# Linear attention beside a spatial gating MLP: moving the attention and its k, v, q projections to other places in the program

## The chip, the cores and the metric

The kernel runs on one core of a Trainium2 chip. The metric is the device time of one execution in microseconds (us). All times come from the chip; spans, waits and clocks come from the profile of one execution each. Every run that is used here counts as a fast run, except the control, of which there is a single run and so no state.

## The reference

```python
def reference(A_x, A_wqkv, A_wo, B_x, B_w_in, B_w_sp, B_b_sp, B_w_out):
    x = A_x                                     # [1, 2048, 576], bf16
    xn = _layernorm(x, axis=-1)
    s = _A_ref(xn, A_wqkv, A_wo)                # attention, 32 heads of 18
    g = _silu(_B_ref(xn, B_w_in, B_w_sp, B_b_sp, B_w_out))
    return x + s * g
# _A_ref: phi(t) = where(t > 0, t + 1, exp(t)) + 1e-6
#   kv = sum_s phi(k) v^T, z = sum_s phi(k); o = phi(q) kv / (phi(q) z + 1e-6); o @ wo
# _B_ref: z = gelu(xn @ w_in); z1, z2 = halves of 2304; z2 = layernorm(z2)
#   g = w_sp @ z2 + b_sp; (z1 * g) @ w_out
```

Two branches share the normalised input and meet only in the last line. Both are stated in bf16.

## The kernel before

The program works on 16 tiles of 128 rows. Its first stage makes, tile after tile, the transposed input `xnT`, the k/v projection (`stage_C`) and the z2 half of the input projection (`stage_D`) with its normalisation (`E1`, `E2`). Then come the sum over all rows (`kvacc`), and the attention by itself: `stage_Q` (q projection), `stage_N` (numerator and denominator), `stage_O`, `stage_R` (transpose) and `stage_W` (times wo). Last comes what is called stage 4 here: z1, g and b. (PSUM, below, is the memory that the matmuls of this program write to, in pieces called banks; SBUF is the one that its other tiles lie in, HBM the one that its inputs, scratch and output lie in.)

```python
    xc0 = ...                                                    # first x chunk, 4 tiles
    load_rows126(nc.sync, Win2[:, :, f0:f0 + fn], ...)           # first of five pieces
    load_rows126(nc.sync, Wkv[:, :, 0:D], A_wqkv, D, 2 * D)
    load_rows126(nc.sync, Wkv[:, :, D:2 * D], A_wqkv, 2 * D, 3 * D)
    for (f0, fn) in fch[1:]:
        load_rows126(nc.sync, Win2[:, :, f0:f0 + fn], ...)
    load_x(1)                                                    # second x chunk
    ...
    for t in range(NS):                                          # NS = 16
        maybe(stage_A1, t + 4)      # statistics of x            (VectorE)
        maybe(stage_A2, t + 3)      # xn                         (VectorE)
        maybe(stage_B, t + 2)       # transposes, xnT            (TensorE, ScalarE)
        maybe(stage_C_pe, t + 1)    # k/v matmuls into one tile of 3 PSUM banks
        maybe(stage_C_act, t + 1)   # Exp, copies of v           (ScalarE)
        maybe(stage_E1, t - 1)      # statistics of z2           (VectorE)
        maybe(stage_E2, t - 2)      # z2 normalised              (VectorE)
        maybe(stage_C_dve, t + 1)   # pk                         (VectorE)
        stage_D(t)                  # 25 z2 matmuls, 5 Gelus     (TensorE, ScalarE)
    ...
    load_rows126(nc.sync, Wqq[:, :, :], A_wqkv, 0, D)            # into a pool opened here
    ...  # kvacc: 5 groups of 16 matmuls, each group evicted before the next
    for j in range(J):                                           # J = 5
        stage_Q(0, j)
    for i in range(NS + 2):
        # stage_Q of the next chunk, N(i), R(i-1), O(i), W(i-2)
        ...
    # stage 4: for each of 4 column chunks z1, g (16 k steps), b; out = x + silu(b) * A_sb
```

Of the kernel before, what the change touches and what calls it, by code (L numbers as in the profile page):

```python
# [28 lines left out]
def kernel(  # L29
# [32 lines left out]
    EPS_LN = 1e-5  # L62

# [3 lines left out]

    consts = ctx.enter_context(tc.tile_pool(name="consts", bufs=1, side="left"))
    big = ctx.enter_context(tc.tile_pool(name="big", bufs=1, side="left"))
    z2p = ctx.enter_context(tc.tile_pool(name="z2p", bufs=1, side="right"))  # L70
# [9 lines left out]
    mask2d = mask[:].rearrange("p a b -> p (a b)")  # L80
    neg_half = consts.tile([P, 1], F32, name="neg_half")
# [3 lines left out]
    z2 = z2p.tile([P, NS, Fh], BF16, name="z2")  # L85
# [4 lines left out]
    pkp_ctx = ExitStack()  # L90
    pkp = pkp_ctx.enter_context(tc.tile_pool(name="pkp", bufs=NS, side="left"))
    p1_sb = ExitStack()
    p1_ps = ExitStack()
    wp1 = p1_sb.enter_context(tc.tile_pool(name="wp1", bufs=1, side="left"))
    Wkv = wp1.tile([P, J, 2 * D], BF16, name="Wkv")
    Win2 = wp1.tile([P, J, Fh], BF16, name="Win2")
    xcp = p1_sb.enter_context(tc.tile_pool(name="xcp", bufs=2, side="left"))
    stg1 = p1_sb.enter_context(tc.tile_pool(name="stg1", bufs=3, side="left"))
    sm1 = p1_sb.enter_context(tc.tile_pool(name="sm1", bufs=6, side="left"))
    ps_t = p1_ps.enter_context(tc.tile_pool(name="ps_t", bufs=1, space=PSUM))  # L100
    ps_kv = p1_ps.enter_context(tc.tile_pool(name="ps_kv", bufs=1, space=PSUM))
    ps_z = p1_ps.enter_context(tc.tile_pool(name="ps_z", bufs=4, space=PSUM))

    fch = _chunks(Fh, 512)
    sch = _chunks(Fh, 384)
# [12 lines left out]
    (f0, fn) = fch[0]  # L118
    load_rows126(nc.sync, Win2[:, :, f0:f0 + fn], B_w_in, Fh + f0, Fh + f0 + fn)
    load_rows126(nc.sync, Wkv[:, :, 0:D], A_wqkv, D, 2 * D)  # L120
    load_rows126(nc.sync, Wkv[:, :, D:2 * D], A_wqkv, 2 * D, 3 * D)
    for (f0, fn) in fch[1:]:
        load_rows126(nc.sync, Win2[:, :, f0:f0 + fn], B_w_in, Fh + f0, Fh + f0 + fn)
    if SC > 1:
        load_x(1)

# [17 lines left out]
    def stage_A2(i):  # L144
        xt, mv, rstd = st_a.pop(i)
        xn = stg1.tile([P, DPAD], BF16, name="xn")
        nc.gpsimd.memset(xn[:, D:DPAD], 0.0)
        nc.vector.tensor_scalar(out=xn[:, 0:D], in0=xt, scalar1=mv[:, 0:1], scalar2=rstd[:, 0:1],
                                op0=ALU.subtract, op1=ALU.mult)
        xn_tiles[i] = xn  # L150
        c, ii = divmod(i, 4)
        if ii == 3 and c + 2 < SC:
            load_x(c + 2)
# [10 lines left out]
    def stage_C_pe(i):  # L164
        pkv = ps_kv.tile([P, 3, 512], F32, name="pkv")
        groups = [(0, 0, 0, 288), (1, 0, 288, 288), (2, 0, D, 4 * GW), (1, 288, D + 4 * GW, JSZ[4])]
        for (b, o, w0, n) in groups:
            for j in range(J):
                nc.tensor.matmul(out=pkv[:, b, o:o + n], lhsT=xnT[0:JSZ[j], j, i * P:(i + 1) * P],  # L169
                                 rhs=Wkv[0:JSZ[j], j, w0:w0 + n], start=(j == 0), stop=(j == J - 1))  # L170
        c_state[i] = pkv

    def stage_C_act(i):
        pkv = c_state[i]
        e = stg1.tile([P, 2, 288], F32, name="e_k")
        nc.scalar.activation(out=e[:], in_=pkv[:, 0:2, 0:288], func=ACT.Exp)
        va = pkp.tile([P, J, GW + 1], BF16, name="va")
        nc.gpsimd.memset(va[:, 0:4, GW:GW + 1], 1.0)
        nc.gpsimd.memset(va[:, 4, JSZ[4]:JSZ[4] + 1], 1.0)
        nc.scalar.copy(out=va[:, 0:4, 0:GW], in_=pkv[:, 2, 0:4 * GW].rearrange("p (j e) -> p j e", j=4))  # L180
        nc.scalar.copy(out=va[:, 4, 0:JSZ[4]], in_=pkv[:, 1, 288:288 + JSZ[4]])
        va_tiles[i] = va
        c_state[i] = (pkv, e)

    def stage_C_dve(i):
        pkv, e = c_state.pop(i)
        nc.vector.tensor_scalar(out=e[:], in0=e[:], scalar1=1.0, scalar2=1e-6, op0=ALU.min, op1=ALU.add)
        pk = pkp.tile([P, D], BF16, name="pk")
        nc.vector.scalar_tensor_tensor(out=pk[:].rearrange("p (b n) -> p b n", b=2), in0=pkv[:, 0:2, 0:288], scalar=0.0,
                                       in1=e[:], op0=ALU.max, op1=ALU.add)  # L190
        pk_tiles[i] = pk

# [10 lines left out]
    def stage_E1(i):  # L203
        st = sm1.tile([P, len(sch), nc.vector.BN_STATS_DIM], F32, name="st3")
        for si, (f0, fn) in enumerate(sch):
            nc.vector.bn_stats(out=st[:, si, :], in_=z2[:, i, f0:f0 + fn])  # L206
        mv = sm1.tile([P, 2], F32, name="mv3")
        nc.vector.bn_aggr(out=mv[:], in_=st[:])
        rstd = sm1.tile([P, 1], F32, name="rstd3")
# [9 lines left out]
    def maybe(fn, i):  # L219
        if 0 <= i < NS:  # L220
            fn(i)

    with tc.high_priority():
        stage_A1(0)
        stage_A2(0)
        stage_B(0)
    for i in range(1, min(4, NS)):
        stage_A1(i)
    for i in range(1, min(3, NS)):
        stage_A2(i)  # L230
    maybe(stage_B, 1)
    stage_C_pe(0)
    stage_C_act(0)
    stage_C_dve(0)
    for t in range(NS):
        maybe(stage_A1, t + 4)
        maybe(stage_A2, t + 3)
        maybe(stage_B, t + 2)
        maybe(stage_C_pe, t + 1)
        maybe(stage_C_act, t + 1)  # L240
        maybe(stage_E1, t - 1)
        maybe(stage_E2, t - 2)
        maybe(stage_C_dve, t + 1)
        stage_D(t)
    stage_E1(NS - 1)
    maybe(stage_E2, NS - 2)
    stage_E2(NS - 1)

    p1_ps.close()
    p1_sb.close()  # L250

    p2_r = ExitStack()
    asbp = ctx.enter_context(tc.tile_pool(name="asbp", bufs=1, side="right"))
    A_sb = asbp.tile([P, NS, D], BF16, name="A_sb")
    bep = p2_r.enter_context(tc.tile_pool(name="bep", bufs=1, side="right"))
    rhsj = bep.tile([P, J, NW], BF16, name="rhsj")
    Wqq = bep.tile([P, J, D], BF16, name="Wqq")
    Wo = bep.tile([P, J, D], BF16, name="Wo")
    pqT = bep.tile([P, J, S], BF16, name="pqT")
    load_rows126(nc.sync, Wqq[:, :, :], A_wqkv, 0, D)  # L260
    load_rows126(nc.sync, Wo[:, :, :], A_wo, 0, D)

    p2_ps = ExitStack()
    ps_q = p2_ps.enter_context(tc.tile_pool(name="ps_q", bufs=2, space=PSUM))

    with tc.tile_pool(name="ps_kvacc", bufs=1, space=PSUM) as ps_kvacc, tc.tile_pool(name="sm2a", bufs=2, side="left") as sm2a:
        kvacc = ps_kvacc.tile([P, J, 512], F32, name="kvacc")
        for j in range(J):
            nj = JSZ[j]
            for i in range(NS):  # L270
                nc.tensor.matmul(out=kvacc[0:nj, j, 0:nj + 1], lhsT=pk_tiles[i][:, j * GW:j * GW + nj],
                                 rhs=va_tiles[i][:, j, 0:nj + 1], start=(i == 0), stop=(i == NS - 1))
            nc.vector.tensor_tensor(out=rhsj[0:nj, j, 0:nj], in0=kvacc[0:nj, j, 0:nj], in1=mask2d[0:nj, 0:nj], op=ALU.mult)
            zc = sm2a.tile([P, 1], F32, name="zc")
            nc.vector.tensor_copy(out=zc[0:nj], in_=kvacc[0:nj, j, nj:nj + 1])
            nc.vector.tensor_scalar(out=rhsj[0:nj, j, nj:nj + JH[j]], in0=mask[0:nj, 0:JH[j], 0], scalar1=zc[0:nj, 0:1], scalar2=None,
                                    op0=ALU.mult)
    pkp_ctx.close()

    spw = ctx.enter_context(tc.tile_pool(name="spw", bufs=1, side="left"))  # L280
    Win1 = spw.tile([P, J, Fh], BF16, name="Win1")
    wT_tiles = {}

    def load_wT(c):
        t = spw.tile([P, NS, 512], BF16, name="wT")
        nc.sync.dma_start_transpose(out=t[:], in_=B_w_sp[c * 512:(c + 1) * 512, :])
        wT_tiles[c] = t

    p2_sb = ExitStack()
    stg2 = p2_sb.enter_context(tc.tile_pool(name="stg2", bufs=3, side="left"))  # L290
    sm2 = p2_sb.enter_context(tc.tile_pool(name="sm2", bufs=4, side="left"))
    ps_nd = p2_ps.enter_context(tc.tile_pool(name="ps_nd", bufs=1, space=PSUM))
    ps_ot = p2_ps.enter_context(tc.tile_pool(name="ps_ot", bufs=2, space=PSUM))
    ps_a = p2_ps.enter_context(tc.tile_pool(name="ps_a", bufs=1, space=PSUM))

    def stage_Q(c, j):
        nj = JSZ[j]
        pq_ps = ps_q.tile([P, 512], F32, name="pq_ps")
        for kt in range(J):
            nc.tensor.matmul(out=pq_ps[0:nj, :], lhsT=Wqq[0:JSZ[kt], kt, j * GW:j * GW + nj],  # L300
                             rhs=xnT[0:JSZ[kt], kt, c * 512:(c + 1) * 512], start=(kt == 0), stop=(kt == J - 1))
        e = stg2.tile([P, 512], F32, name="e_q")
        nc.scalar.activation(out=e[0:nj, :], in_=pq_ps[0:nj, :], func=ACT.Exp)  # L303
        nc.vector.tensor_scalar(out=e[0:nj, :], in0=e[0:nj, :], scalar1=1.0, scalar2=1e-6, op0=ALU.min, op1=ALU.add)  # L304
# [173 lines left out]
```

## Time and profile before

| | before |
|---|---|
| median of the first 4 runs | 612.01 us (610.53 to 612.80) |
| span of the profiled run (610.53 us) | 608.8 us |
| mean granted TensorE clock in it | 0.994 |
| TensorE / VectorE / ScalarE busy | 584.2 / 253.0 / 209.0 us |
| moved by DMA | 27.14 MB |

The profile is of one run, here the fastest of the four. That matters when its span is set against a median.

Two readings bear on the argument and are not in the prediction. The first is of the seam between first stage and attention. In the chain of waits (start, length, what held the end), VectorE finishes the last z2 tile, and then the load of the q weights is on the path for 4.41 us: its buffer came free only there.

```profile
142.31 0.89 DVE z L216
...
143.33 4.41 DMA Wqq<-in_A_wqkv_dram
```

The timeline of TensorE (PE) at the same place (start, length, engine, line, form; in brackets the idle time before and what ended it) shows PE waiting between the groups of kvacc:

```profile
140.23 1.08 PE L271 MATMUL kvacc<-va,pk 128*126 128x127 bf16 x16 [0.47 <-ACT z L199]
143.69 1.84 PE L271 MATMUL kvacc<-va,pk 128*126 128x127 bf16 x16 [2.38 <-DVE zc L275]
...
149.03 0.81 PE L300 MATMUL pq_ps<-xnT,Wqq 126*126 126x512 bf16 x3
```

The second reading is of the groups of instructions on ScalarE. The loads of function tables (count, then busy us and ns of one, then idle time before) are many, but they lie on an engine that is not the bound:

```profile
L199 ACT ACT_TABLE_LOAD x16 | 20.5, 1283 | 0.3
L176 ACT ACT_TABLE_LOAD x15 | 19.2, 1283 | 0.3
```

### The profile page before, as it was taken

The page shows a single profiled execution, that of the slowest core. Times are in us where ns is not written, and L with a number is a line of the kernel's source. Part 1 is how long each engine was busy: PE and PEld are TensorE (multiplying, and loading weights), DVE is VectorE, ACT ScalarE, POOL GpSimd, SP SyncE. Part 2 cuts the span into 40 slices and gives each one's busy share as a digit, 9 for nine tenths or more (in the row PEclk, how much of TensorE's full clock was granted, in tenths as well). Part 3 has the DMA queues.
Part 4 walks back from the last instruction along what each step waited for, and adds up shares of the span by engine and source line. Part 5 has one row for each costly group of instructions (what it writes and reads, how often), then busy time and mean ns, then how long its engine had stood idle before and what let it go on. Part 6 is the DMA issues. An engine that isn't in the chain of part 4 may idle for free.

```text
span 608.8 us, 8283 instructions
## 1 busy us (share of the span) xinstructions
PE 584.2 (96%) x3468; PEld 321.2 (53%) x3468; DVE 253.0 (42%) x552; ACT 209.0 (34%) x325; POOL 26.7 (4%) x105
## 2 busy tenths in 40 slices
PE   3799999997899999999999999999999999999996
PEld 2455555555577644444754444574444475444465
DVE  4599777775776203323211332230233321123323
ACT  1799999982465550000242000135000024300011
POOL 3023000000001000000000000000000000000000
PEclk9999999998999999999999999999999999999999
DMA  8410000003910150000710000530000071000001
GB/s 247 132 39 2 1 2 1 0 2 91 290 23 1 56 193 1 1 1 1 177 40 1 0 1 0 118 88 12 0 1 1 1 176 41 1 1 0 1 0 40
DMA packets 48153, 27.14 MB, mean 45 GB/s; under 512 B 33780, under 2 KB 47412, under 8 KB 48116
## 3 DMA queue, kind: packets, MB, share of 16 engines
q1 hardware_dynamic: 48116, 26.61, 16.1%
q8 instruction: 27, 0.44, 0.3%
q14 instruction: 10, 0.08, 0.0%
HBM read 15.86 MB, written 2.36 MB: 30 GB/s over the span
## 4 chain that ended last, share of the span: by engine, by line
PE 91%; DVE 3%; issue 2%; DMA 2%; ACT 1%; POOL 0%; SPq 0%; POOLq 0%; ACTq 0%
PE g_ps L425 40%; PE z_ps L403 13%; PE b_ps L439 12%; PE zp L197 11%; PE pkv L169 7%; PE a_ps L360 3%; PE pq_ps L300 3%; PE pT L159 1%; DMA xc<-in_A_x_dram 1%; PE oT_ps L350 1%; PE nd L318 1%; DVE pqT L305 1%; DMA Wqq<-in_A_wqkv_dram 1%; DVE e_q L304 0%; ACT e_q L303 0%
## 5 line engine op out<-in xcount | busy, mean ns | idle before, releaser
L425 PE MATMUL g_ps<-wT,z 128*128 128x512 bf16 x1152 | 250.1, 379 | 0.0
L425 PEld LDWEIGHTS <-z 128*128 128x128 bf16 x1152 | 112.7, 98 | 135.8
L427 DVE TENSOR_TENSOR gb<-g_ps,b_bc 128x512 bf16<-128x512 f32 x72 | 49.8, 691 | 232.9 <-PE g_ps L425 207.6
L406 ACT ACTIVATE z<-z_ps 128x512 bf16<-128x512 f32 x72 | 42.6, 597 | 215.1 <-PE z_ps L403 215.0
L197 PE MATMUL zp<-Win,xnT 126*128 126x512 bf16 (+3 forms) x400 | 81.8, 358 | 0.0
L403 PE MATMUL z_ps<-xnT,Win 126*128 126x512 bf16 (+1 forms) x360 | 80.6, 379 | 0.2 <-DVE pqT L305 0.2
L439 PE MATMUL b_ps<-Wout,z 128*128 128x288 bf16 x576 | 71.2, 286 | 0.0
L439 PEld LDWEIGHTS <-z 128*128 128x128 bf16 x576 | 56.3, 98 | 15.0
L403 PEld LDWEIGHTS <-Win 126*128 126x128 bf16 (+1 forms) x360 | 34.9, 97 | 42.1 <-issue 0.8
L197 PEld LDWEIGHTS <-xnT 126*128 126x128 bf16 (+1 forms) x400 | 37.5, 97 | 36.9 <-issue 0.4
L206 DVE BATCH_NORM_STATS2 st<-z 128x6 f32<-128x384 bf16 x96 | 46.5, 549 | 13.0 <-ACT z L199 12.8
L169 PE MATMUL pkv<-Wkv,xnT 126*128 126x288 bf16 (+4 forms) x320 | 44.8, 296 | 3.2 <-DVE rstd L138 3.2
L199 ACT ACTIVATE z<-zp 128x512 bf16<-128x512 f32 (+1 forms) x80 | 40.9, 555 | 5.7 <-PE zp L197 5.3
L169 PEld LDWEIGHTS <-xnT 126*128 126x128 bf16 (+1 forms) x320 | 28.6, 101 | 18.8 <-issue 4.9
L444 DVE TENSOR_TENSOR sB<-sB,A_sb 128x576 f32<-128x576 f32 x16 | 12.1, 758 | 56.5 <-ACT sB L442 56.5
L428 DVE TENSOR_TENSOR z<-gb,z 128x512 bf16<-128x512 bf16 x72 | 30.6, 425 | 7.1
L442 ACT ACT_TABLE_LOAD x4 | 5.1, 1283 | 76.5 <-PE b_ps L439 76.5
L300 PE MATMUL pq_ps<-xnT,Wqq 126*126 126x512 bf16 (+3 forms) x100 | 24.5, 380 | 1.9 <-DVE pqT L305 1.6
L442 ACT ACTIVATE sB<-b_ps 128x576 f32<-128x576 f32 x16 | 10.4, 651 | 40.0 <-PE b_ps L439 32.5
L360 PE MATMUL a_ps<-Wo,oT 126*128 126x288 bf16 (+1 forms) x160 | 22.5, 285 | 0.0
L199 ACT ACT_TABLE_LOAD x16 | 20.5, 1283 | 0.3
L159 PE MATMUL pT<-ident,xn 128*126 128x128 bf16 x80 | 9.7, 232 | 10.4 <-POOL rstd L139 9.6
(58 smaller groups left out, 345.1 us busy)
## 6 DMA issues: line engine op xcount, KB each, us to landing
Wout<-in_B_w_out_dram SPq DMA_DIRECT2D x1, 2592.0 KB
x_r<-in_A_x_dram SPq DMA_DIRECT2D x16, 144.0 KB
out_dram<-ot SPq DMA_DIRECT2D x16, 144.0 KB
Win<-in_B_w_in_dram SPq DMA_DIRECT2D x1, 2268.0 KB
Win<-in_B_w_in_dram SPq DMA_DIRECT2D x4, 504.0 KB
xc<-in_A_x_dram SPq DMA_DIRECT2D x3, 576.0 KB
Wkv<-in_A_wqkv_dram SPq DMA_DIRECT2D x2, 567.0 KB
Wqq<-in_A_wqkv_dram SPq DMA_DIRECT2D x1, 567.0 KB
```

The costliest lines, as they stand in the source:

```text
L169: nc.tensor.matmul(out=pkv[:, b, o:o + n], lhsT=xnT[0:JSZ[j], j, i * P:(i + 1) * P], rhs=Wkv[0:JSZ[j], j, w0:w0 + n], start=(j == 0), stop ...
L197: nc.tensor.matmul(out=zp[:, 0:fn], lhsT=xnT[0:JSZ[j], j, i * P:(i + 1) * P], rhs=Win2[0:JSZ[j], j, f0:f0 + fn], start=(j == 0), stop=(j = ...
L199: nc.scalar.activation(out=z2[:, i, f0:f0 + fn], in_=zp[:, 0:fn], func=ACT.Gelu_apprx_tanh)
L206: nc.vector.bn_stats(out=st[:, si, :], in_=z2[:, i, f0:f0 + fn])
L300: nc.tensor.matmul(out=pq_ps[0:nj, :], lhsT=Wqq[0:JSZ[kt], kt, j * GW:j * GW + nj], rhs=xnT[0:JSZ[kt], kt, c * 512:(c + 1) * 512], start=( ...
L360: nc.tensor.matmul(out=a_ps[:, hh, 0:288], lhsT=oT[0:JSZ[j], j, :], rhs=Wo[0:JSZ[j], j, hh * 288:(hh + 1) * 288], start=(j == 0), stop=(j ...
L403: nc.tensor.matmul(out=zp[:], lhsT=Win1[0:JSZ[j], j, ft * P:(ft + 1) * P], rhs=xnT[0:JSZ[j], j, c * 512:(c + 1) * 512], start=(j == 0), st ...
L406: nc.scalar.activation(out=z1[:], in_=zp[:], func=ACT.Gelu_apprx_tanh)
L425: nc.tensor.matmul(out=gp[:], lhsT=z2[:, k, ft * P:(ft + 1) * P], rhs=wT[:, k, :], start=(k == 0), stop=(k == NS - 1))
L427: nc.vector.tensor_tensor(out=gb[:], in0=gp[:], in1=b_bc[:, c * 512:(c + 1) * 512], op=ALU.add)
L428: nc.vector.tensor_tensor(out=z1t[ft][:], in0=gb[:], in1=z1t[ft][:], op=ALU.mult)
L439: nc.tensor.matmul(out=bp[:, hh, 0:288], lhsT=z1t[ft][:, si * P:(si + 1) * P], rhs=Wout[:, ft, hh * 288:(hh + 1) * 288], start=(ft == 0), ...
```

## The change

The intent is fivefold: have the k/v projection and the q projection run ahead of everything that needs the large `Win2`, so that the start needs fewer bytes; do all Exp work before all Gelu work, so that ScalarE need not change function tables within each tile; put the attention of tile i beside the z2 matmuls of tile i; keep exponentials in bf16; and start the first tile sooner, with warming matmuls ahead. To make room in SBUF, the attention's result goes to a scratch tensor in HBM and comes back in stage 4. The core of the diff:

```diff
     load_rows126(nc.sync, Wkv[:, :, 0:D], A_wqkv, D, 2 * D)
     load_rows126(nc.sync, Wkv[:, :, D:2 * D], A_wqkv, 2 * D, 3 * D)
-    (first Win2 piece ahead of Wkv, four pieces after it)
     if SC > 1:
         load_x(1)
+    load_rows126(nc.sync, Wqq[:, :, :], A_wqkv, 0, D)
+    load_x(2)
+    load_x(3)
...
-        pkv = ps_kv.tile([P, 3, 512], F32, name="pkv")
+        pa = ps_kv.tile([P, 512], F32, name="kvb")     # pb, pc alike; five banks
...
-        e = stg1.tile([P, 2, 288], F32, name="e_k")
+        e = stg1.tile([P, 2, 288], BF16, name="e_k")   # e_q alike
...
+    with tc.manual_schedule(engines={mybir.EngineType.DVE, mybir.EngineType.PE}):
+        warm(10)
+        stage_A1(0)
+        stage_A2(0)
+        stage_B(0)
+        warm(2)
+        (stage_A1 of tiles 1 and 2, stage_A2 of tile 1)
+    (the five Win2 pieces, then Wo)
+    for t in range(NS):
+        maybe(stage_A1, t + 3)
+        maybe(stage_A2, t + 2)
+        maybe(stage_B, t + 1)
+        stage_C_pe(t)
+        stage_C_act(t)
+        (stage_Q of the chunk before)
+        stage_C_dve(t)
+    for j in range(J):
+        stage_Q(SC - 1, j)
+    (kvacc: all five groups, then one batched eviction)
...
-        nc.scalar.copy(out=A_sb[:, i, :].rearrange("p (h n) -> p h n", h=2), in_=a_ps[:, :, 0:288])
+        a_sb = asp.tile([P, 2, 288], F32, name="a_sb")
+        nc.scalar.copy(out=a_sb[:], in_=a_ps[:, :, 0:288])
+        nc.scalar.dma_start(out=a_scr[i * P:(i + 1) * P, :], in_=a_sb[:].rearrange("p h n -> p (h n)"))
...
     for i in range(NS + 2):
+        maybe(stage_D, i)
+        maybe(stage_E1, i - 1)
+        maybe(stage_N, i)
+        maybe(stage_E2, i - 2)
+        maybe(stage_R, i - 1)
+        maybe(stage_O, i)
+        maybe(stage_W, i - 2)
```

## The prediction

> **What bounds the kernel now.** I read the page's busy row and slices first, then a windows view cut where the program changes stage, then the chain of waits in order of time, then the timeline of the start.
>
> ```profile
> PE 584.2 (96%) x3468; PEld 321.2 (53%) x3468; DVE 253.0 (42%) x552; ACT 209.0 (34%) x325; POOL 26.7 (4%) x105
> ...
> PE   3799999997899999999999999999999999999996
> ```
>
> TensorE (PE) is busy 96% of the span. All slices but the first two, the tenth, eleventh and the last show a full digit, so what can be won lies in the start and around slices 10 and 11. The columns of the windows view are stretch, length, then busy time per engine:
>
> ```profile
> 0.00:11.85 11.85, 1.49 (x11) 1.35 (x12) 6.66 (x21) 1.98 (x2) 5.03 (x49) 1.00 0.79 233
> 11.85:36.13 24.28, 21.03 (x127) 11.83 (x126) 14.19 (x40) 16.83 (x27) 3.23 (x8) 0.93 0.44 125
> 36.13:127.60 91.47, 91.47 (x598) 52.45 (x596) 72.58 (x172) 83.19 (x132) 13.10 (x29) 1.00 0.03 8
> 127.60:148.30 20.70, 17.12 (x123) 10.93 (x121) 13.90 (x35) 10.72 (x18) 1.94 (x6) 0.92 0.17 50
> 148.30:211.65 63.35, 60.88 (x556) 43.05 (x555) 40.99 (x110) 34.97 (x55) 3.40 (x13) 1.00 0.34 86
> 211.65:290.45 78.80, 78.80 (x366) 35.69 (x366) 20.10 (x36) 10.59 (x18) 0.00 (x0) 1.00 0.14 46
> ```
>
> In the long first stage (36 to 128 us) PE is busy 91.47 of 91.47 us although ScalarE (ACT) is busy 83.19: ACT is nearly full but not the bound. From 211.65 on (z1, g, b) PE is full as well, and the change leaves that work alone. The chain of waits gives the true pace of each piece, since there each piece ends where the next begins:
>
> ```profile
> 59.05 2.47 PE pkv L169 x20
> 61.52 4.33 PE zp L197 x20
> 65.91 0.55 PE zp L197 x5
> 66.69 2.47 PE pkv L169 x20
> ...
> 148.27 0.92 PE kvacc L271 x16
> ...
> 173.13 0.34 PE oT_ps L350 x5
> 173.47 1.23 PE a_ps L360 x10
> 174.71 1.08 PE pq_ps L300 x5
> ```
>
> One first-stage tile takes 66.69 - 59.05 = 7.64 us: k/v 2.47, z2 4.88, transposes 0.29. The timeline of the start shows a wait that is not the data's: the scale of the first x tile is ready at 4.86 us, yet VectorE (DVE) first finishes the statistics of three more tiles, which came at 6.29.
>
> ```profile
> 4.31 0.55 POOL L139 TENSOR_TENSOR rstd<-rstd,neg_half 128x1 f32<-128x1 f32 x1 [2.75 <-DVE rstd L138]
> ...
> 9.10 2.64 DVE L148 TENSOR_SCALAR xn<-xc,mv,rstd 128x576 bf16<-128x576 bf16 x4
> 9.58 0.79 PE L159 MATMUL pT<-ident,xn 128*126 128x128 bf16 x5 [9.58 <-POOL rstd L139]
> ...
> 26.67 4.01 PE L169 MATMUL pkv<-Wkv,xnT 126*128 126x288 bf16 x20 [3.25 <-DVE rstd L138]
> ```
>
> [...] the 20 k/v matmuls after the 3.25 us gap took 4.01 us where they take 2.47 later. [...] g has a mean of 379 ns, but 250.1 us over 1152 is 217 ns each; so I count start to start. [...] 1283 ns a load; the trace has 1283 on every load. [...] the z2 normalisation does 2304 bf16 columns in 879 ns, the f32 e_k step 576 in 456. So I put e_k and e_q in bf16 at about 0.22 us of issue each (an estimate from the 879).
>
> **The change, part by part.** The build of the changed kernel gives the new order on each engine. The stages become: (1) k/v and Q for all tiles; (2) kvacc; (3) z2 of tile i together with N, R and W of the attention; (4) z1, g, b as before.
>
> The same matmuls stay (12 warming ones are added). Their pace from the chain: transposes and k/v 16 x (0.29 + 2.47) = 44.2; Q 20 x 1.08 = 21.6; kvacc 5 x 0.92 = 4.6; the new loop 16 x (4.88 + N, R, W), where before one such turn with a Q takes 3.03 us (174.71 to 177.74), so N+R+W = 1.95, hence 16 x 6.83 = 109.3. Sum 179.7 us.
>
> Where does stage 4 start? Before, from 211.65 to 603.93 PE works without a gap, but ten z and fourteen g matmuls lay ahead of 211.65: 24 x 0.217 = 5.2, so the equivalent start is 206.4. The start and all waits ahead of it cost 206.4 - 179.7 = 26.7 us: first k/v matmul at 11.6; about 6 us in 11.85 to 36.13 (late second x chunk, cold clock); about 5 at kvacc, which waited on the last gelus, on its evictions group by group, and on Wqq's load; about 4 where attention alone was too thin (two Q buffers, exp, two DVE steps in series, and the last A eviction plus table load before z1's gelus).
>
> Removed and no gain by itself: 31 alternating Exp and Gelu table loads (15 + 16, 39.8 us of ACT). They lay beside a PE that was full. The f32 scratch copy of A adds 16 x 288 KB out and back; it lies beside long matmul stretches and A is needed 80 us later. The final multiplication stays a DVE operation into f32, so its 758 ns should stay.
>
> New start. DVE now normalises tile 0 right after its rstd: 4.86 + 0.45, transposes at about 5.4 instead of 9.58[...]. The first k/v matmuls then wait for Wkv: 1.25 MB come before its K half is complete, so I put them at about 8. But DVE binds next: its new order puts the statistics of tiles 3 to 5 ahead of the k work of tile 0, and tile 4 belongs to the second x chunk. That chunk needs 2.5 MB moved; before, 5.16 MB were in at 23.05 and the first slice ran at 247 GB/s, so I estimate it at 12 us. From there to the release of the first k bank DVE has 6 statistics (0.365 each), 2 normalisations (0.35), e_k, half a pk (0.38) and small steps: about 4.3 us, so the third bank of tile 1's k/v starts near 16.3, after an idle PE of some 3.5 us, and therefore cold. With five banks at three a tile, each of tiles 2 to 4 again waits for half a pk of the tile before; stepping through DVE's order gives waits of 0.3 to 0.8 each and an end of tile 4's k/v near 28.1. Fourteen microseconds of its work are done by then (5 x 2.47 + 6 x 0.29), so start and waits cost 14.0. After that Q adds 1.08 us of PE per tile, DVE needs about 3 of 3.8 us, and PE is full.
>
> Boundaries: kvacc waits for the last Q's exp and two DVE steps (1.75) behind five z2 matmuls (1.08) and some slack: 0.8. The rhsj chain (about 2 us) lies behind ten z2 matmuls (1.6): 0.3. The last W to z1: 0.2. [...] start and waits come to 15.8. Stage 4 then starts at 179.7 + 15.8 = 195.5 instead of 206.4: 10.9 us less, 612.0 - 10.9 = 601.1, say 601.
>
> **The rivals.** (a) The start goes better: the x chunk lands at 10 to 11 instead of 12, PE stays warm. Start and waits fall to 12 or 13: 597.5 to 599, over 2% (12.2 us). For it: SyncE has fewer transfers ahead of it than before, and the DMA was only 79% busy in the first 11.85 us. Against it: DVE's new order is long whatever the DMA does. (b) The ACT queue becomes a new wait: each A tile's store is issued from ACT with two a_sb buffers, and z2 has three banks instead of four. If ACT stands for its store, gelus come late and PE stops each turn; 0.4 us a turn would give 607. Against it: ACT has 2.8 + 0.7 + 0.6 + an issue of about 0.4 in 6.83 us, and a store has a whole turn to land. (c) ACT's table loads were holding PE all along and the gain is far larger. Against it: 91.47 of 91.47. (d) The k/v stage becomes bound by DVE for all tiles: 16 x 0.5 more, 608. Against it: about 3 of 3.8 us once Q is in.
>
> **Range and chances.** (a) takes the time to 597.5, a mild (b) or (d) to 605. The two per cent line (599.8) needs start and waits of at most 14.5; my sum is 15.8 with an uncertainty of about 3. So faster by over 2% gets 0.34, within 2% 0.65, slower 0.01.
>
> **What would show it.** Right: stage 4 takes the same time as before; one turn of the z2 and attention loop takes 6.8 us with PE full; one table load at the first gelu; PE idle gathered ahead of about 28 us, ended by DVE pk, with the second x chunk landing near 12 us and a lower clock after it. Wrong: PE gaps inside the loop ended by ACT (b), waits for pk through the whole k/v stage (d), or no wait for the x chunk (a). If stage 4 itself changed length, the whole sum is wrong.

## The result, and the profile after

| | before | after |
|---|---|---|
| median of the runs of the same rounds | 612.79 us (16 runs, 610.53 to 615.01) | 598.46 us (11 runs, 595.59 to 600.18) |
| ratio, with its 95% interval | | 0.976 (0.9741 to 0.9779): faster |
| span of the profiled run | 608.8 us (run of 610.53) | 596.5 us (run of 598.25) |
| TensorE / VectorE / ScalarE busy | 584.2 / 253.0 / 209.0 us | 585.3 / 243.7 / 173.5 us |
| moved by DMA | 27.14 MB | 36.58 MB |

Ratios, here and below, are the mean time of one kernel's fast runs over that of the other's fast runs of the same rounds, so they are not quite the ratio of the medians that are quoted. The experiments ran in other rounds than the two kernels, and the median of the kernel before lay between 611.28 and 612.79 us from one set of rounds to the next; so small differences between versions of different sets are read from the ratios, not from the times.

The windows view of the kernel after, cut at its changes of stage (stretch, length, busy time of PE, of its weight loads, of VectorE, ScalarE and GpSimd, then granted clock, DMA share, GB/s):

```profile
0.00:27.48 27.48, 21.95 (x143) 12.59 (x144) 19.19 (x73) 12.24 (x26) 10.20 (x62) 0.94 0.93 245
27.48:83.70 56.22, 55.57 (x387) 35.18 (x385) 36.36 (x98) 33.21 (x77) 3.37 (x12) 1.00 0.07 18
83.70:90.24 6.54, 6.54 (x101) 5.76 (x102) 2.04 (x8) 3.79 (x6) 0.22 (x2) 1.00 0.05 13
90.24:191.36 101.12, 101.12 (x744) 60.70 (x743) 80.14 (x204) 59.57 (x103) 10.27 (x29) 1.00 0.27 85
191.36:197.76 6.40, 6.40 (x42) 3.77 (x41) 1.34 (x4) 3.98 (x7) 0.55 (x1) 1.00 0.39 115
197.76:591.62 393.86, 393.77 (x2073) 202.26 (x2070) 103.14 (x174) 60.07 (x93) 0.00 (x0) 1.00 0.18 49
```

The rows are: start up to the end of the fifth tile's k/v; the rest of k/v and q; kvacc; z2 beside attention; the seam; stage 4. From 83.70 us on PE is busy in every row for all but 0.09 us. Against the prediction's windows of before, the holes of 3.58 us (127.60 to 148.30) and 2.47 us (148.30 to 211.65) are gone. What is left lies in the first row, and 0.65 us in the second.

The chain of waits in the loop of z2 and attention shows one turn from z2 to z2, 123.09 - 116.27 = 6.82 us:

```profile
116.27 4.88 PE zp L302 x25
...
121.86 1.23 PE a_ps L375 x10
123.09 4.88 PE zp L302 x25
```

The timeline of the start answers to the one in the prediction:

```profile
8.07 0.90 PE L181 MATMUL kvb<-Wkv,xnT 126*128 126x288 bf16 x6 [0.95 <-DMA Wkv<-in_A_wqkv_dram]
...
13.51 0.46 DVE L145 BATCH_NORM_STATS2 st<-xc 128x6 f32<-128x288 bf16 x1 [3.54 <-DMA xc<-in_A_x_dram]
...
17.25 0.44 DVE L202 SCALAR_TENSOR_TENSOR pk<-kvb,e_k 128x288 bf16<-128x288 f32 x1
...
17.74 4.18 PE L181 MATMUL kvb<-Wkv,xnT 126*128 126x288 bf16 x20 [2.31 <-DVE pk L202]
```

The first tile is transposed at 5.53 us instead of 9.58 and its k/v begins at 8.07 instead of 11.64. Then VectorE stands still for 3.54 us until the second x chunk lands at 13.51, the first half of pk comes at 17.25, and TensorE, which waited 2.31 us for it, works cold afterwards: 4.18 us for 20 matmuls. *Cold* means that matmuls take longer than the same ones do later (20 of k/v take 2.63 us from 22.07 on). The windows view gives a granted clock of 0.50 of the full one from 18 to 20 us here. It does not show every cold stretch: the ten warming matmuls at the start took 4.45 us, 0.445 each where g takes 0.217 at the same 512 columns, and the granted clock of 0.00 to 5.50 us reads 1.00.

**Where the time came from.** I call *equivalent start of stage 4* the moment at which stage 4 would have begun if none of its matmuls had been done ahead. Before it is 206.4 us (in the prediction). After, 15 z and one g matmul were done before 197.76: 197.76 - 16 x 0.217 = 194.3. With the same 179.7 us of work ahead of it, start and waits fell from 26.7 to 14.6 us. They split at the end of the start:

| start and waits ahead of stage 4 | before | after | gained |
|---|---|---|---|
| start (before: up to 36.13 us, less 18.6 of work; after: up to 27.48, less 14.1) | 17.5 | 13.4 | 4.1 |
| all that follows, up to stage 4 | 9.2 | 1.2 | 8.0 |
| sum | 26.7 | 14.6 | 12.1 |

The 18.6 are 3 k/v of 2.47, 2 z2 of 4.88 and 5 transposes of 0.29; the 14.1 are 5 k/v and 6 transposes. The spans differ by 12.3 us, so the table holds all but 0.2 of it. The medians differ by 14.3 us, and the remaining 2 us are the control's subject.

### The profile page after: what moved, and what is told of

Its sections match the earlier page's. It is cut to its first block, busy times and chain, and to the rows that moved or that the text cites. A ratio compares the mean times of both kernels' runs of the same rounds, so it can differ in the third digit from the quotient of the medians.

```text
span 596.5 us, 8342 instructions
## 1 busy us (share of the span) xinstructions
PE 585.3 (98%) x3480; PEld 320.3 (54%) x3480; DVE 243.7 (41%) x560; ACT 173.5 (29%) x310; POOL 24.6 (4%) x105
## 2 busy tenths in 40 slices
DMA packets 52761, 36.58 MB, mean 61 GB/s; under 512 B 34292, under 2 KB 47924, under 8 KB 52724
## 4 chain that ended last, share of the span: by engine, by line
PE 96%; DVE 1%; issue 1%; DMA 1%; POOL 0%; ACT 0%; SPq 0%; POOLq 0%; ACTq 0%
PE g_ps L440 42%; PE z_ps L414 13%; PE zp L302 13%; PE b_ps L454 12%; PE kvb L181 6%; PE pq_ps L210 4%; PE a_ps L375 3%; PE oT_ps L365 1%; PE nd L333 1%; DMA xc<-in_A_x_dram 1%; PE kvacc L264 1%; PE pT L169 1%; POOL rstd L151 0%; DVE st L145 0%; DVE st L146 0%
## 5 line engine op out<-in xcount | busy, mean ns | idle before, releaser
L311 DVE BATCH_NORM_STATS2 st<-z 128x6 f32<-128x384 bf16 x96 | 51.3, 552 | 12.3 <-ACT z L304 11.5
L304 ACT ACTIVATE z<-zp 128x512 bf16<-128x512 f32 (+1 forms) x80 | 43.4, 554 | 31.8 <-PE zp L302 31.8
L181 PE MATMUL kvb<-Wkv,xnT 126*128 126x288 bf16 (+4 forms) x320 | 44.0, 292 | 4.1 <-DVE pk L202 2.3
L459 DVE TENSOR_TENSOR sB<-sB,a_r 128x576 f32<-128x576 f32 x16 | 12.1, 758 | 56.5 <-ACT sB L457 50.7
L457 ACT ACT_TABLE_LOAD x4 | 5.1, 1283 | 72.6 <-PE b_ps L454 72.6
L321 DVE TENSOR_SCALAR z<-z,mv,rstd 128x2304 bf16<-128x2304 bf16 x16 | 14.0, 874 | 9.3 <-POOL rstd L316 9.3
L375 PEld LDWEIGHTS <-oT 126*128 126x128 bf16 (+1 forms) x160 | 15.0, 97 | 3.6
```

The source lines that it names most:

```text
L181: nc.tensor.matmul(out=pt[:, o:o + n], lhsT=xnT[0:JSZ[j], j, i * P:(i + 1) * P], rhs=Wkv[0:JSZ[j], j, w0:w0 + n], start=(j == 0), stop=(j ...
L304: nc.scalar.activation(out=z2[:, i, f0:f0 + fn], in_=zp[:, 0:fn], func=ACT.Gelu_apprx_tanh)
L311: nc.vector.bn_stats(out=st[:, si, :], in_=z2[:, i, f0:f0 + fn])
L375: nc.tensor.matmul(out=a_ps[:, hh, 0:288], lhsT=oT[0:JSZ[j], j, :], rhs=Wo[0:JSZ[j], j, hh * 288:(hh + 1) * 288], start=(j == 0), stop=(j ...
```

## The experiments

The theory to test: the start gains because less must be loaded before TensorE has steady work, and the middle because the attention no longer runs alone behind a late load; table loads, scratch and bf16 are worth nothing by themselves. The rivals: the tables held TensorE; the batched eviction or the warming made the gain; the scratch cost something. A measure that is free of the varying start helps: I call *interior* the time from the first q matmul to the end of the last b matmul. In the kernel after it is 564.22 us and begins at 27.32.

### The kernel before once more

No edit.

> The kernel before, unchanged, for a second profile. The first profile of it had a span of 608.8 us in a run of 610.5, while the median of its runs is 612.8. Theory: the two microseconds between the profiled run and the median lie in the start, where loads arrive at a time that varies, so stage 4 (z1, g, b) takes 392.3 + 5.2 us again within 0.5 and the rest varies. Rival: the pace of TensorE itself differs by run (a clock of 0.991 instead of 0.994), then stage 4 differs by about 1.3 us.

612.33 us (one run), span 610.6. From the timeline of TensorE in this run:

```profile
10.94 5.01 PE L169 MATMUL pkv<-Wkv,xnT 126*128 126x288 bf16 x20
...
27.17 4.96 PE L169 MATMUL pkv<-Wkv,xnT 126*128 126x288 bf16 x20 [3.17 <-DVE rstd L138]
```

The first k/v took 5.01 us (3.81 in the first profile) and the third 4.96 (4.01). The steady part began at 37.86 instead of 36.13, and from there to the end of the last b matmul it took 567.75 us against 567.72. The whole difference of 1.8 us thus lies in the start, and it comes from slower matmuls: the two k/v are 1.20 and 0.95 us longer and the z2 after them 0.28, while the first k/v began 0.70 us earlier; the mean granted clock of the run is 0.991 against 0.994. If this run is typical, the kernel before loses some 2 us more in its start than the run whose profile I had read, and with 4.1 + 1.8 + 8.0 = 13.9 us nearly the whole of the measured 14.3 is placed. That it is typical is not shown: its time is close to the median of 612.79 in the rounds of the result, but in its own rounds the median of the kernel before was 611.28, a full microsecond less.

### z2 for all tiles first, attention alone after it

```diff
     for i in range(NS + 2):
         maybe(stage_D, i)
         maybe(stage_E1, i - 1)
-        maybe(stage_N, i)
         maybe(stage_E2, i - 2)
-        maybe(stage_R, i - 1)
-        maybe(stage_O, i)
-        maybe(stage_W, i - 2)
+    for i in range(NS + 2):
+        maybe(stage_N, i)
+        (stage_R, stage_O, stage_W)
```

> The changed kernel with its middle loop cut in two: first z2 of all tiles, then the attention (N, R, O, W) of all tiles by itself. Everything else stays, Q and the table loads too. Theory: the gain ahead of stage 4 comes mostly from laying the attention, which alone is bound by the round trip nd, DVE, transposes, beside z2; a turn of attention alone then takes 2.2 to 2.4 us instead of 1.95, so 4 to 7 us are lost: 602 to 606. Rival: the gain comes from Q's and kvacc's new place or from the start; then the time stays within 1.5 us of the changed kernel, 597 to 600.

599.78 us, ratio 0.9814 (0.9777 to 0.9850); the interior is 566.94, so 2.7 us longer. That is less than the 4 to 7 I expected and more than the 1.5 of the rival; by its time alone the run lies in the rival's range of 597 to 600, with a first q matmul at 25.14 us. Two things happened. The scheduler drew z1 matmuls of stage 4 into the holes of the attention, and z2 by itself became bound by VectorE. The chain of waits there runs over the statistics of z2, 140.55 - 135.64 = 4.91 us a tile:

```profile
135.64 2.77 DVE st L311 x6
...
139.67 0.88 DVE z L321
140.55 2.78 DVE st L311 x6
```

TensorE would need 4.88 for the same tile, so that this costs little by itself. Pairing z2 with attention is worth about 2.7 us, not more, since other work fills the holes of the attention as well.

### No table loads in the first stage of before

```diff
-            nc.scalar.activation(out=z2[:, i, f0:f0 + fn], in_=zp[:, 0:fn], func=ACT.Gelu_apprx_tanh)
+            nc.scalar.activation(out=z2[:, i, f0:f0 + fn], in_=zp[:, 0:fn], func=ACT.Exp)
```

> The kernel before with Exp in place of the gelu of z2, so that the 31 alternating table loads of its first stage go (the result is wrong on purpose). Theory: the loads lay beside a TensorE that was full, so the time stays within 1.5 us of the kernel before (ratio 0.997 to 1.003). Rival: ScalarE, 91% busy there, held TensorE back; then up to 10 us go.

610.01 us (20 runs), ratio 0.9974 (0.9959 to 0.9989); the result is wrong on purpose. About 1.6 us (0.0026 x 611.3; by the interval 0.7 to 2.5) of 14 may come from the tables: little, but not nothing. Where they are gained is not shown; the run that was profiled took 611.55 us. The windows view of this kernel in its first stage says why it is not more:

```profile
38.00:139.00 101.00, 101.00 (x648) 56.68 (x647) 82.14 (x193) 58.13 (x117) 14.50 (x31) 1.00 0.02 7
```

ScalarE is busy 58.13 of 101 us where it was busy 83.19 of 91.47 in before, and TensorE is full in both. The rival, a TensorE held for up to 10 us, falls.

### Another order of the first four turns

The order of statement is now enforced on three engines through the fourth tile, and the group of v that shares a bank with k comes ahead of the large one. The table of Exp is loaded at the start, and the early load of the table of Gelu is left out.

```diff
-        groups = [(pa, 0, 0, 288), (pb, 0, 288, 288), (pc, 0, D, 4 * GW), (pb, 288, D + 4 * GW, JSZ[4])]
+        groups = [(pa, 0, 0, 288), (pb, 0, 288, 288), (pb, 288, D + 4 * GW, JSZ[4]), (pc, 0, D, 4 * GW)]
...
+    nc.scalar.preload_act_table(ACT.Exp)
-    with tc.manual_schedule(engines={mybir.EngineType.DVE, mybir.EngineType.PE}):
+    with tc.manual_schedule(engines={..., mybir.EngineType.Activation}):
         ...
+        for t in range(4):
+            kv_turn(t)          # the body of the k/v loop
...
-    nc.scalar.preload_act_table(ACT.Gelu_apprx_tanh)
```

> The changed kernel with another order in the first four turns of the k/v stage, fixed on DVE, ACT and PE: the k work of tile t comes ahead of the statistics of tile t+4, the two exps of a tile come ahead of the copy of v, the column group of v that shares k's bank comes ahead of the large v group, and the Exp table is loaded at the start. In the changed kernel's trace DVE stood 3.5 us for the second x chunk with k's work of tile 0 behind that wait in its order, then PE stood 2.3 us for pk, and then ran 20 matmuls in 4.18 us at the low clock instead of 2.47. Theory: DVE's order is the cause, PE is no longer held, tile 4's k/v ends near 24 us instead of 27.5: 3 to 4 us less than the changed kernel, about 595. Rival: the late x chunk itself is the cause, then at most 1 us is won.

595.14 us (five runs, 594.23 to 595.70), ratio 0.9726 (0.9699 to 0.9752). This is the fastest version measured, though its rounds did not include the kernel after, whose interval reaches down to 0.9741. The wait for pk is gone and the first q matmul comes at 25.14 instead of 27.32 us; the interior is 563.85. The gain is 2 to 3 us where I had expected 3 to 4. It rests on the times of the runs (the kernel after took 595.59 to 600.18): one profile could not show it, since the split, with the start of the kernel after, had its first q matmul at 25.14 us too. Which of the edits gave it was not separated. What is left is that now the v half of the weights is waited for, as the timeline shows after an earlier wait of 1.30 us at 11.84:

```profile
12.32 1.26 PE L181 MATMUL kvb<-Wkv,xnT 72*128 72x72 bf16 x6 [0.19 <-DMA Wkv<-in_A_wqkv_dram]
```

### The old order of the start, without warming

```diff
-        warm(10)
         stage_A1(0)
-        stage_A2(0)
-        stage_B(0)
-        warm(2)
-        (statistics of tiles 1 and 2, xn of tile 1)
+        (statistics of four tiles, then xn of three, then the transposes of tile 0)
```

The order is also no longer enforced there (`high_priority` in place of `manual_schedule`), and VectorE looks one tile further ahead.

> The changed kernel with the start of the kernel before on DVE (statistics of tiles 0 to 3 ahead of the normalisation of tile 0, one tile more of look-ahead) and without the twelve warming matmuls; loads as in the changed kernel. Theory: in the changed kernel PE is held at about 15 us by k's work behind the second x chunk anyway, so tile 0's head start of 4 us and the warming are mostly lost there: at most 1.5 us slower than the changed kernel (598 to 600). Rival, as the prediction's working had it in part: the earlier first transposes are what the start gains, then about 4 us are lost: 602 to 603.

597.42 us, ratio 0.9750 (0.9731 to 0.9768): nothing is lost. The first transposes come at 8.04 us instead of 5.53, and the first k/v runs wholly cold, in 5.01 us where the third takes 2.63 (the mean granted clock of this run reads 1.000),

```profile
10.20 5.01 PE L181 MATMUL kvb<-Wkv,xnT 126*128 126x288 bf16 x20
```

yet no wait for pk follows and the first q matmul comes at 26.50. So the head start of tile 0 and the warming matmuls together bought no time. In the kernel after, VectorE spent 3.54 us of that head start waiting for the second x chunk; here it waited 1.35. The warming was not taken out alone.

### All of Win2 ahead of the second x chunk

```diff
     load_rows126(nc.sync, Wkv[:, :, D:2 * D], A_wqkv, 2 * D, 3 * D)
+    for (f0, fn) in fch:
+        load_rows126(nc.sync, Win2[:, :, f0:f0 + fn], B_w_in, Fh + f0, Fh + f0 + fn)
     if SC > 1:
         load_x(1)
```

> The changed kernel with the loads in the order of the kernel before: all of Win2 ahead of the second x chunk, which then arrives at about 23 us instead of 13. DVE's order, rebuilt for that, has the k work of tiles 0 to 3 ahead of the wait. Theory: the k/v work of four tiles is done by about 21 us, so only the wait for the chunk, its statistics and a cold clock are lost, 2 to 4 us against the changed kernel: 600 to 602. Rival: the place of the x chunk in the queue is the whole of the start's gain and all ten microseconds of its delay are lost: 606 to 609.

604.44 us, ratio 0.9866 (0.9844 to 0.9888): 6 to 6.5 us lost, about twice what I expected. The timeline of VectorE shows the chunk landing at 24.77 us,

```profile
24.77 0.46 DVE L147 BATCH_NORM_STATS2 st<-xc 128x6 f32<-128x288 bf16 x1 [9.34 <-DMA xc<-in_A_x_dram]
```

and that of TensorE shows what it did to the fifth tile:

```profile
27.59 0.80 PE L171 MATMUL pT<-ident,xn 128*126 128x128 bf16 x5 [8.87 <-DVE rstd L152]
```

TensorE idles for 8.87 us, then starts cold: five transposes take 0.80 us where the ones at 13.31 us took 0.47, and the first five q matmuls 2.34 us where they take 1.27 in the kernel after. In this kernel, whose first stage needs only x and small weights, the place of x in the queue was worth more than any other detail of the start that was tried.

### kvacc evicted group by group

```diff
+            nc.vector.tensor_tensor(out=rhsj[0:nj, j, 0:nj], in0=kvacc[0:nj, j, 0:nj], ...)
+            nc.vector.tensor_copy(out=zc[0:nj, j:j + 1], in_=kvacc[0:nj, j, nj:nj + 1])
+            nc.vector.tensor_scalar(out=rhsj[0:nj, j, nj:nj + JH[j]], ...)
-        (the batched eviction behind all five groups)
```

> The changed kernel with kvacc evicted group by group as in the kernel before, instead of all five groups' matmuls first and then one eviction. Theory: each group's matmuls wait for the DVE steps on the group before (in the kernel before this wait was 0.45 us where DVE was free, 2.38 where it had the last z2 work first), four waits of 0.5 to 0.7, less what the shorter chain after the last group gives back: 1 to 2.5 us slower than the changed kernel. Rival: the z2 matmuls that may be laid between fill all of it, then the same within 0.7 us.

597.08 us, ratio 0.9758 (0.9730 to 0.9786); interior 564.87, 0.65 us more. One wait between groups is left, 0.45 us before the second:

```profile
83.29 1.09 PE L264 MATMUL kvacc<-va,pk 128*126 128x127 bf16 x16 [0.45 <-DVE zc L267]
```

After it z2 matmuls run between the groups. The rival was right here: what removed the waits at kvacc is other work that is ready, not the batching.

### The attention's result kept in SBUF

```diff
-        a_sb = asp.tile([P, 2, 288], F32, name="a_sb")
-        (copy to a_sb, store to a_scr; load of a_r in stage 4)
+        nc.scalar.copy(out=A_sb[:, i, :].rearrange("p (h n) -> p h n", h=2), in_=a_ps[:, :, 0:288])
```

> The changed kernel with A kept on the chip in bf16 (18 KB a partition, it fits) instead of being written to device memory in f32 and read back. Theory: the round trip lies beside matmuls everywhere but at the last W, where ACT stood 0.8 us for a store to free a buffer and no PE wait followed; so the same time within 0.7 us. Rival: the stores and loads slow other transfers or ACT somewhere on the path; then 1 us or more is won.

599.55 us (595.81 to 601.07), ratio 0.9774 (0.9747 to 0.9801), no clear difference. The interior is 564.22, the same to the hundredth: the scratch costs nothing. The profiled run was long because of its start, which has the same order as the kernel after:

```profile
18.86 4.96 PE L180 MATMUL kvb<-Wkv,xnT 126*128 126x288 bf16 x20 [2.52 <-DVE pk L201]
```

Its first q matmul came at 29.83 us. With this start code I have seen it between 25.14 (in the split) and 29.83. The chunk's arrival is one part of the spread (the statistics that wait for it began at 14.64 us here and at 12.55 in the split); the pace of the matmuls after the wait for pk is another, for in the split, after a wait of 2.15 us, the same 20 took 2.62 us and not 4.96 (the mean granted clock is 0.999 there and 0.991 here):

```profile
16.77 2.62 PE L181 MATMUL kvb<-Wkv,xnT 126*128 126x288 bf16 x20 [2.15 <-DVE pk L202]
```

### The kernel before with the q weights loaded early

```diff
     if SC > 1:
         load_x(1)
+    load_rows126(nc.sync, Wqq[:, :, :], A_wqkv, 0, D)      # in a pool of its own
...
-    load_rows126(nc.sync, Wqq[:, :, :], A_wqkv, 0, D)      # behind the first stage
```

To make room, `A_sb` moves to a pool that is opened after kvacc.

> The kernel before with Q's weights loaded at the start instead of after the z2 stage (A's buffer moves to the other side of the memory to make room). In the kernel before, kvacc stands 2.4 us for its eviction, which DVE does behind the last z2 statistics and normalisations, and the Q weights' load is only issued at 143.3 us and ends at 147.7. Theory: with the weights there, Q matmuls of the first chunk fill part of these waits and the load's wait goes: 1 to 3 us faster than the kernel before. Rival: DVE's z2 work alone sets when anything of the attention can start, then the time stays within 0.7 us.

606.98 us, ratio 0.9904 (0.9872 to 0.9935): 5.9 us gained (0.0096 x 612.6; by the interval 4.0 to 7.8), about twice the most that I expected. z2 ended at 141.54 us instead of 139.76, since this run had a slow start; from there to the end of the last b matmul it took 458.48 us where the first profile of before has 464.09. That is 5.6 less, or 5.4 without the one q matmul that had been done ahead. The timeline of TensorE at kvacc:

```profile
142.95 1.47 PE L302 MATMUL pq_ps<-xnT,Wqq 72*126 72x512 bf16 x6
145.52 1.09 PE L271 MATMUL kvacc<-va,pk 128*126 128x127 bf16 x16 [1.11 <-DVE zc L275]
...
149.28 1.08 PE L271 MATMUL kvacc<-va,pk 128*126 128x127 bf16 x16
```

q matmuls now stand between the groups of kvacc, as there is something to do while VectorE evicts, and the clock stays up (1.00 from 138 to 150 us): kvacc's four wide groups take 1.08 to 1.09 us each. Of the 8.0 us that the change gains in the middle, this one load in its place accounts for about 5.4; the split (second experiment) lost 2.7 in the other direction. Their sum is 8.1, which fits, though the two were measured in different programs.

### The kernel before with the second x chunk ahead of four Win2 pieces

```diff
+    if SC > 1:
+        load_x(1)
     for (f0, fn) in fch[1:]:
         load_rows126(nc.sync, Win2[:, :, f0:f0 + fn], B_w_in, Fh + f0, Fh + f0 + fn)
-    if SC > 1:
-        load_x(1)
```

> The kernel before with one edit: the second x chunk is loaded ahead of four of the five Win2 pieces instead of behind them. Theory: the wait at 23.4 to 26.7 us (and the low clock after it, 4.0 to 4.9 us for 20 matmuls instead of 2.5) goes, the Win2 pieces come 2 us later and z2 of tile 0 waits somewhat for them: 2 to 5 us faster than the kernel before, that is, most of the start's part of the change. Rival: the late Win2 pieces hold PE as long as the late x chunk did; then within 1 us.

612.02 us (20 runs, one of them of 3515 us, not a fast run and so not in the ratio), ratio 0.9989 (0.9976 to 1.0002): the same. The profiled run shows it in more detail than expected:

```profile
138.28 1.08 PE L271 MATMUL kvacc<-va,pk 128*126 128x127 bf16 x16 [0.47 <-ACT z L199]
...
147.82 1.49 PE L300 MATMUL pq_ps<-xnT,Wqq 126*126 126x512 bf16 x3
```

kvacc begins at 138.28 us, where the first profile of before has 140.23 and the control 141.95, so the order does help the start. But at kvacc the load of the q weights is still late, the clock stays low for longer (0.74 from 139 to 152 us, where before has 0.87), and three q matmuls that took 0.81 us in before take 1.49. By 152 us all but 0.2 of the 2 us is lost. So a gain in the start was given back at the next wait. One profile shows this; that it happens in most runs is only inferred from the medians. The kernel before with this edit and the early q weights together, the cheap cure of both holes, was not run.

### Exponentials in f32 again

```diff
-        e = stg1.tile([P, 2, 288], BF16, name="e_k")
+        e = stg1.tile([P, 2, 288], F32, name="e_k")     # e_q alike
```

> The changed kernel with e_k and e_q in f32 as in the kernel before. Measured from the first Q matmul of the trace to the end of the last b matmul (564.2 us in the changed kernel), so that the start does not blur it. Theory: DVE has 3 of 3.85 us per turn, the 0.3 us more stay hidden, and that stretch is the same within 0.3 us. Rival: DVE or the release of the k banks is near the path; then 1 us or more is lost over the twelve turns with Q.

597.99 us, ratio 0.9778 (0.9744 to 0.9813), no difference within the interval. The first q matmul came at 26.00 us, the interior is 564.94, 0.7 more. By this profile bf16 exponentials are worth about a microsecond at most; the theory of 0.3 us at most does not hold, and the rival of 1 us or more is not reached.

### The best start with a single load of the k and v weights

Against the version with the new order of the first four turns:

```diff
-    load_rows126(nc.sync, Wkv[:, :, 0:D], A_wqkv, D, 2 * D)
-    load_rows126(nc.sync, Wkv[:, :, D:2 * D], A_wqkv, 2 * D, 3 * D)
+    load_rows126(nc.sync, Wkv[:, :, :], A_wqkv, D, 3 * D)
```

> The reordered start of the fourth experiment, and k's and v's weights loaded as one transfer with rows of 2304 bytes instead of two with rows of 1152. There the v half landed at 12.3 us and PE stood 1.5 us for it; the transfer engines were over 90% busy in the first 27 us. Theory: half as many rows take less time, the weights are complete at about 10.5, and the second x chunk comes earlier too: 1 to 2 us less than the fourth experiment, a ratio of 0.970. Rival: the transfers are bound by bytes, then the k half comes later than now by what the v half gains and nothing is won.

598.44 us, ratio 0.9770 (0.9747 to 0.9794): slower than the two loads by some 2.7 us (0.0044 x 612), the intervals just overlapping. The interior is 564.22, about the same; the first q matmul comes at 26.71 instead of 25.14.

```profile
9.80 4.96 PE L180 MATMUL kvb<-Wkv,xnT 126*128 126x288 bf16 x20 [1.17 <-DMA Wkv<-in_A_wqkv_dram]
```

The first k/v waits for the whole of the weights until 9.80 us, after idle gaps of 1.57 and 1.17 us, and then runs cold for all of its 20 matmuls, in 4.96 us, where the split load let the first ten run from 9.14 us in 1.40. I did not separate the later landing from the slower matmuls (the mean granted clock is 0.992 here and 1.000 with the two loads). The theory of a gain of 1 to 2 us fails.

## Why the prediction was right, and where it was not

The predicted 601.0 us lies 2.5 us above the median of 598.46, which is inside the range. The kernel came out 2.4% faster, past the two per cent line to which I had given 0.34. For that line the prediction asked for start and waits of at most 14.5 us; they were 14.6, so that the line was passed through the reference point (last in this list) and not through the sum. Its steps, one by one:

- **The work ahead of stage 4, 179.7 us.** Right. A turn of the loop takes 6.82 to 6.83 us as predicted, and kvacc 4.46 instead of 4.6. q takes 1.11 us in the chain instead of 1.08, 0.6 us over 20. Stage 4 is unchanged: 392.19 us of PE in 392.28 before, 393.77 in 393.86 from a slightly earlier cut after.
- **The stage-4 start at 195.5 us.** It was 194.3.
- **The start at 14.0 us.** It was 13.4, but its parts were further off than the sum, so that the near match is in part luck. k/v began at 8.07 as predicted (8). The x chunk came at 13.51, not 12. Its delay did not cost what it should have: tile 1 ran all of its k/v from 12.49 without waiting, and the wait for pk fell on tile 2 at 17.74. The further waits of 0.3 to 0.8 us on tiles 3 and 4 did not occur. The wait for pk was 2.31 us, where I had about 3.5. I had bound the third bank of tile 1 to the first bank of tile 0; the trace shows tile 1 done before that bank was read by the pk step at 17.25.
- **Tile 0 first and warming.** The working credited the new order with the earlier k/v. That is true of the k/v and worth nothing in time: without tile 0 first and without the warming matmuls the kernel took 597.42 us.
- **The boundaries at 1.8 us.** Of these 0.5 us were an allowance of mine, drawn from no trace. The boundaries took 1.2: 0.65 at kvacc (predicted 0.8) and none at the rhsj chain (0.3) or the seam to stage 4 (0.2). The rest is the slower q above.
- **What the seam of before cost.** The working gave about 5 us to kvacc and 4 to the thin attention, 9 in all, against 9.2 in the table. The experiments fit the sum (8.1 for the 8.0 gained) and shift the shares: 5.4 hang on the late q weights alone, and group-by-group eviction is worth at most 0.65 once other work is ready.
- **Tables and scratch are worth nothing.** Nearly right: about 1.6 us (0.7 to 2.5) for the tables, measured in the kernel before, and 0.00 of the interior for the scratch. The sign named for the tables, one load at the first gelu, came at 83.79 us.
- **The reference point.** Here the number was missed most. 612.0 - 10.9 took a gain computed from a profiled run of 610.53 us off a median of 612.0. Of the four runs known then it was the fastest; the control starts 1.8 us worse, and as the run of after that I read was close to its median (598.25 against 598.46), the change seems to gain that as well. The remaining shortfall is 12.1 - 10.9 = 1.2 us, from the start (0.6) and the boundaries (0.6).

Of the rivals, (a), a better start, gave the range into which the time fell, but neither its sum nor its cause came: start and waits were 14.6 us and not 12 or 13, the x chunk landed later, not sooner, and TensorE did go cold. (By the working's own numbers 12 or 13 makes 597.3 to 598.3, and (d) 609; these slips do not touch its sum.) The queue of ScalarE (b) cost nothing: the issue of a store took 0.33 us there, the longest wait that a store caused there was 0.8 us, once, and TensorE never waited for it. (c) is refuted by the kernel without tables, and (d) by the second row of the windows after, 55.57 of 56.22 us.

## What to carry to other kernels

When one engine is full nearly all the time (here 584.2 of 608.8 us), a large rearrangement gains only what its few holes hold, so measure the holes first and look for the cheapest cure of each: a load moved to the start gave 5.9 us where the whole change gave 14.3. A gain in a start can be given back at the next wait, through the clock, as one profile here shows (0.74 of the full one from 139 to 152 us, against 0.87), so follow it to a point where the engine is full before counting it. And profile the kernel before more than once: the spread of its start was as large as some of the effects in question.

## What the traces show of gaps, pace and table loads

- After some idle gaps of TensorE its matmuls were slower: 3.25 us in the kernel before (20 k/v matmuls in 4.01 us after it), 2.31 us in the kernel after (4.18 us), 2.52 us in the one without scratch (4.96 us), and, in the first k/v of the f32 experiment, 1.81 us (six matmuls in 1.37 us, which took 0.90 in the kernel after, behind a gap of 0.95). After gaps of 2.15 us in the split, 2.17 with kvacc by groups and 1.58 in the f32 experiment they were not (2.62 us for 20 each). So the length of one gap did not decide it; what did is not shown. The pace at the start varied from run to run too: ten warming matmuls took 4.45 us in the kernel after and 3.91 in the one without scratch.
- In the kernel before g takes 250 us for 1152 matmuls of 512 columns, 217 ns each. The weight loads leave no gap beside them: in stage 4 of the kernel after TensorE is busy 393.77 of 393.86 us, with 202.26 us of weight loads in the same stretch.
- A load of a function table takes 1283 ns in the profiles of before and after. The idle time before the 16 and the 15 loads of the first stage of before is 0.3 us each in sum, and none shows behind the one that was looked at: it ends at 64.10 us and its gelu begins at 64.11.
- The start of a kernel spreads: with one and the same start code the first q matmul came between 25.14 and 29.83 us, and the whole kernel took 595.59 to 600.18 us.
